# Fused causal convolution and soft mixture of experts on one core: phi's copies, the first halos, unread products, expert layers and first stores reordered

## The chip, the cores and the metric

One core of a Trainium2 chip runs the whole program. The metric is the device time in microseconds (us) of one execution, given as the median of several runs. Lower is better. The engines are PE (matrix products), DVE (vector), ACT (scalar and activation), POOL (GpSimd) and SP, which here only issues transfers; 16 DMA engines move the data. All data are fp32.

## What is computed

```python
# B, S, D = 8, 3584, 192; 8 heads of 24 channels, 7 taps; E = 8 experts, 4 slots each, F = 1024
w = softmax(weight, axis=-1)                        # one 7-tap filter per head
x_unf = x_pad[:, idx, :].reshape(B, S, K, H, group) # causal windows of 7 rows
x = einsum('hk,bskhg->bshg', w, x_unf).reshape(B * S, D)

logits = x @ phi                                    # 28672 x 32
d = softmax over the tokens (axis 0)                # dispatch weights
slot_input = (d.T @ x).reshape(E, S_per_e, D)
for e in range(E):
    slot_out[e] = maximum(slot_input[e] @ w1[e], 0.0) @ w2[e]
c = softmax over the slots (axis 1)                 # combine weights
out = c @ slot_out.reshape(n_slots, D)
```

The softmax over all 28,672 tokens stands between the convolution of every batch and the first row of the output.

## The kernel before

The eight batches of 3584 tokens lie in five buffers `rb[0..4]` of 128 partitions. A batch is 32 blocks of 112 tokens (two halves of 56, each with 8 rows of the block before it, the halo); it is loaded in four quarters of 8 blocks. `load_x` (L251) issues the transfers and then copies the halo rows of each quarter from partitions 64 on to partitions 0 on (`halo`, L272); the copy runs on ACT for two quarters of batch 0 and on POOL otherwise.

The convolution is a product with a banded matrix `toep` per head. DVE builds the bands (`bprod`, L351, a product of 392 columns, and `bsum`, L354), POOL takes the products of heads 3 and 6. A convolution group (`conv`, L408) is written to one of four PSUM pairs and evacuated over its own input (L196 on ACT, L200 on DVE). For batches 0 and 1 a group covers two heads and half of the blocks, first quarters 0 and 1, then 2 and 3; for the others one head and all blocks, which needs all four halos. DVE then transposes the result in blocks of 32 (`turn`, L452) into `xt`.

Batches are taken in units of two. The logits of a unit are six steps (`step`, L492), which need `phi4`: phi lies on 32 partitions and is copied to the other 96 by three copies (`phi_copies`, L287 to L289). The steps stand between the convolution groups of the next unit. Behind them come the evacuation with a running minimum (L517), the exponential (L532), a transpose on PE (L558) and the dispatch product (L583), whose results are merged into `acc` on DVE (L590). The combine weights are made per batch by `rows` (L601): two transposes and two reductions on DVE, two products of 1.7 us on POOL (L610), one exponential on ACT.

`filler(n)` (L432) adds n products of the identity with itself (L438, two instructions each in the order) into a PSUM pair that is about to be overwritten; nobody reads them.

When the last dispatch is done, slot sums become slot inputs `s1z`, `s2z` (L746 to L763); the first expert layer `l1` (L786) is taken in two halves h of 512 columns, each from a high part (`s1z`, L789) and a low part (`s2z`, L793); then ReLU (L802 on ACT, L804 on DVE), a transpose `ht` of each quarter q (L816) with its copy, the second layer `l2` (L827), a gather (L845) and the copy to `so` (L848). The weights are loaded into `rb[3]`, `rb[4]` (w1), `xt` and `rb[0]` (w2) once their former contents have been read (L717 to L733).

The output of a batch is made for tokens k and k + 1 of every seven at a time (L870), evacuated by ACT and DVE, one half each, and stored by four transfers per batch (`st`, L895); batch 0 is stored in two portions of four.

The order on each engine is set by `Plan` (L16 to L148): each step has a cost in us, keys that it reads and writes, and a priority; `order` places the steps at the earliest time by these costs, and among those that are ready the one of the lowest priority value first. Steps with `chain=True` keep the order in which they are added. The engines run what stands in this order, and each instruction waits for what it needs.

## Time and profile before

| | us |
|---|---|
| median of 3 runs | 212.44 (212.21 to 212.63) |
| the profiled execution | 213.65 |
| its span, first to last instruction | 211.3 |
| PE busy | 176.9 (84%) |
| DVE busy | 153.7 (73%) |
| ACT busy | 100.1 (47%) |
| POOL busy | 77.8 (37%) |

The span is what lies between the first and the last instruction on the core; 2.35 us of the profiled execution lie around it. The profile comes from one execution, so durations read from it are set against 213.65, not against the median. The views read here are the page's busy tenths (the span in 40 slices of 5.28 us), the timeline of one engine, in which equal instructions in a row are merged, and the table of stretches. A row of the timeline gives the start, the time from the first start to the last end, the engine, the line, the operation, its tiles, and in brackets how long the engine had been idle and what released it.

### The profile page before, as it was taken

How to read it: one execution, taken by the hardware profiler on the slowest of the kernel's cores; microseconds unless marked ns; L12 is line 12 of the kernel's file. 1: busy time of each engine (PE TensorE's matmuls, PEld its weight loads, DVE VectorE, ACT ScalarE, POOL GpSimd, SP SyncE). 2: the span in 40 equal slices, each digit the busy share in tenths (PEclk: the TensorE clock that was granted, in tenths of full speed). 3: DMA queues.
4: the chain of work that ended last, by engine and by line, in shares of the span. 5: the costliest groups of instructions: out<-in, count | busy, mean ns of one | idle time of the engine just before them, and what ended most of it. 6: DMA issues, size and time to landing. Idle time of an engine off the chain costs nothing. (4 is left out here: it accounts for less than half of the span.)

```text
span 211.3 us, 6138 instructions
## 1 busy us (share of the span) xinstructions
PE 176.9 (84%) x2632; PEld 109.0 (52%) x2632; DVE 153.7 (73%) x231; ACT 100.1 (47%) x156; POOL 77.8 (37%) x69
## 2 busy tenths in 40 slices
PE   7749999999999999999999989988999999680000
PEld 3235786427632375323646667333898988660000
DVE  5994797088997999978889967769789897660000
ACT  3083655075284563747882080331669779550000
POOL 7726646655345640654000602246303633300000
PEclk9978999999999999999999999999999887875555
DMA  5999999997799917999079699900199999999994
GB/s 166 326 322 326 323 330 323 325 326 238 208 330 324 310 30 218 326 380 236 21 229 304 159 352 379 356 26 0 39 337 324 399 413 401 416 412 416 415 413 193
DMA packets 46124, 60.08 MB, mean 284 GB/s; under 512 B 1682, under 2 KB 38418, under 8 KB 46098
## 3 DMA queue, kind: packets, MB, share of 16 engines
q1 hardware_dynamic: 45888, 59.68, 86.0%
q8 instruction: 20, 0.33, 0.7%
q10 hardware_dynamic: 210, 0.02, 0.1%
q14 instruction: 6, 0.05, 0.1%
HBM read 37.68 MB, written 22.02 MB: 282 GB/s over the span
## 5 line engine op out<-in xcount | busy, mean ns | idle before, releaser
L196 ACT COPY rb<-ps 128x768 f32<-128x768 f32 (+1 forms) x97 | 69.4, 783 | 50.7 <-PE ps L408 28.6
L452 DVE STREAM_TRANSPOSE xt<-rb 128x1024 f32<-128x1024 f32 (+1 forms) x60 | 57.4, 1004 | 9.4 <-ACT rb L196 6.6
L198 POOL COPY rb<-rb 8x1536 f32<-8x1536 f32 x30 | 43.7, 1457 | 40.2 <-DMA rb<-in_x_dram 39.3
L408 PE MATMUL ps<-rb,toep 64*64 64x384 f32 (+1 forms) x640 | 48.2, 432 | 5.3 <-ACT rb L196 5.3
L610 POOL TENSOR_TENSOR eb<-eb,rms 128x896 f32<-128x896 f32 x16 | 27.0, 1696 | 61.2 <-DVE rms L614 43.5
L870 PE MATMUL ps<-so,eb 32*128 32x192 f32 x448 | 38.8, 454 | 3.1 <-DVE eb L627 1.7
L870 PEld LDWEIGHTS ps<-so,eb 32*128 32x128 f32 x448 | 35.0, 318 | 7.0 <-ACT rb L196 3.3
L408 PEld LDWEIGHTS ps<-rb,toep 64*64 64x64 f32 x640 | 22.0, 134 | 30.4 <-issue 20.2
L200 DVE COPY rb<-ps 128x768 f32<-128x768 f32 (+1 forms) x31 | 25.7, 854 | 6.5 <-ACT rb L196 3.3
L492 PE MATMUL ps<-xt,phi 32*32 32x384 f32 (+1 forms) x768 | 27.4, 545 | 0.0
L583 PE MATMUL ps<-rb,xt 128*32 128x192 f32 x448 | 19.0, 327 | 0.0
L617 DVE TENSOR_REDUCE rms<-eb 128x28 f32<-128x896 f32 x16 | 16.9, 1060 | 1.9 <-ACT eb L623 1.9
L492 PEld LDWEIGHTS ps<-xt,phi 32*32 32x32 f32 x768 | 11.1, 103 | 12.6 <-issue 7.5
L583 PEld LDWEIGHTS ps<-rb,xt 128*32 128x32 f32 x448 | 14.1, 110 | 4.0 <-ACT rb L196 0.3
L438 PE MATMUL ps<-ident 128*128 128x256 f32 x48 | 14.0, 423 | 0.0
L532 ACT ACTIVATE xt<-eb,nmr 128x896 f32<-128x896 f32 x8 | 8.3, 1044 | 9.2 <-DVE eb L517 9.1
L438 PEld LDWEIGHTS ps<-ident 128*128 128x128 f32 x48 | 8.8, 200 | 4.8 <-issue 2.5
L558 PEld LDWEIGHTS ps<-ident,xt 128*128 128x128 f32 x64 | 6.9, 141 | 5.4 <-ACT xt L532 3.6
L196 ACT COPY xt<-ps 128x512 f32<-128x512 f32 (+2 forms) x12 | 6.1, 529 | 7.4 <-DVE xt L200 6.0
L558 PE MATMUL ps<-ident,xt 128*128 128x128 f32 x64 | 8.7, 280 | 1.1 <-ACT xt L532 1.1
L627 DVE STREAM_TRANSPOSE eb<-eb 128x896 f32<-128x896 f32 x8 | 8.8, 1106 | 0.1
L620 DVE STREAM_TRANSPOSE eb<-eb 128x896 f32<-128x896 f32 x8 | 8.6, 1087 | 0.0
(89 smaller groups left out, 114.7 us busy)
## 6 DMA issues: line engine op xcount, KB each, us to landing
out_dram<-rb SPq DMA_DIRECT2D x28, 672.0 KB, 9.6
rb<-in_x_dram SPq DMA_DIRECT2D x24, 768.0 KB, 9.5
rb<-in_x_dram SPq DMA_DIRECT2D x8, 672.0 KB, 7.3
rb<-in_moe_w_dram SPq DMA_DIRECT2D x4, 1024.0 KB, 10.4
xt<-in_moe_w_dram SPq DMA_DIRECT2D x4, 768.0 KB, 7.9
rb<-in_moe_w_dram SPq DMA_DIRECT2D x4, 768.0 KB, 10.7
rb<-in_moe_w_dram SPq DMA_DIRECT2D x4, 512.0 KB, 13.7
out_dram<-rb SPq DMA_DIRECT2D x4, 384.0 KB, 5.0
```

The costliest lines, as they stand in the source:

```text
L196: nc.scalar.copy(dst, src)
L198: nc.gpsimd.tensor_copy(dst, src)
L200: nc.vector.tensor_copy(dst, src)
L408: nc.tensor.matmul(dst[:, :, h * CG : (h + 1) * CG], toep[r, h0 + h, :], rb[i][r, lo + g : lo + n : 2, ch], start=True, stop=True,)
L438: lambda e: nc.tensor.matmul(prs[p][:, 0, 0 : 2 * P].rearrange("p (r n) -> p r n", n=P), ident, ident.unsqueeze(1).broadcast_to((P, 2, P)) ...
L452: nc.vector.transpose(xt[:, s, k, lo : lo + n], rb[i][:, lo : lo + n, 32 * k : 32 * k + 32])
L492: nc.tensor.matmul(q[a % 2][32 * c : 32 * c + 32, a // 2, 0 : m * U * n].rearrange("p (s u j) -> p s u j", s=m, j=n), phi4[sl, k, :], xt[s ...
L558: nc.tensor.transpose(q[:, u // 4, (u % 4) * P : (u % 4 + 1) * P], t[:, u].rearrange("p g t -> p (g t)"), ident)
L583: nc.tensor.matmul(q[32 * c : 32 * c + 32, 0, 0:D], d[:, u, 32 * c : 32 * c + 32], rb[i][:, U * c + u, :], start=(u == 0), stop=(u == U - 1),)
L610: return lambda e: veng(e).tensor_tensor(out=ev, in0=ev, in1=rb_, op=op)
L617: return lambda e: nc.vector.tensor_reduce(out=rm, in_=ev, axis=AX.X, op=op)
L870: nc.tensor.matmul(q4[c // 2][:, c % 2, (q - k) * D : (q - k + 1) * D], cb[:, :, q], so[sl, :], start=True, stop=True, tile_position=(32 * ...
```

## The change

- phi's copies to the other partitions are added behind batch 0's stage and also wait for the evacuation of batch 0's last heads; their priority goes from -2 to 12.
- Batch 0's halos of quarters 0 and 1 are on ACT (before: 1 and 2); quarters 2 and 3 on POOL.
- Fewer fillers: in the first two batches 2, 2, 2, 0 | 0, 0, 0, 2 | 0, 0, 0, 3 | 0, 0, 0, 1 (before 2, 3, 2, 1 | 0, 0, 0, 1 | 0, 0, 0, 4 | 0, 0, 0, 2), none among the first unit's logits (2), three before the last logits (4), one after the last dispatch (3).
- The expert layers are chained on PE in an order written by hand, the first layer cut into its high and low part.
- Batch 0 is stored in portions of two and five tokens (before four and three). One planned wait of two w1 loads is dropped.

```diff
--- before.py
+++ after.py
@@ -273,7 +273,7 @@
                 copy(e, rb[i][0:HR, n * q : n * (q + 1), :], rb[i][64 : 64 + HR, n * q : n * (q + 1), :])
 
             add(fn, {"DMA": n * P * D * 4 / 325e3 + (0.6 if b == q == 0 else 0)}, writes=[ldk[i][q]], after=hk[i] + [hak[i][q]], prio=pr)
-            add(halo, {"ACT": 1.5} if b == 0 and q in (1, 2) else {"POOL": 1.5}, reads=[ldk[i][q]] + ([f"z{i}"] if q == 0 else []), writes=[hak[i][q]], prio=pr)
+            add(halo, {"ACT": 1.5} if b == 0 and q < 2 else {"POOL": 1.5}, reads=[ldk[i][q]] + ([f"z{i}"] if q == 0 else []), writes=[hak[i][q]], prio=pr)
 
     def load_w(dst, src, nbytes, key, after, prio):
         add(lambda e: nc.sync.dma_start(dst, src), dma(nbytes), writes=[key], after=after, prio=prio)
@@ -332,8 +332,7 @@
     )
 
     add(w_norm, {"DVE": 0.9}, reads=["wb"], writes=["wb"], prio=-50)
-    add(phi_copies, {"ACT": 1.05}, reads=["phi0"], writes=["phi4"], prio=-2)
-
+    
     def shifts(e):
         lo, k = 2 * HR - ZS, T - HR + ZS
         nc.vector.tensor_tensor(out=shf[:, 0:k], in0=ident[:, 66 : 66 + k], in1=ident[:, lo : lo + k], op=ALU.add)
@@ -462,7 +461,7 @@
             for lo in (0, NI):
                 for h in range(0, H, 2):
                     conv(b, h, 2, lo, NI)
-                    filler(((2, 3, 2, 1), (0, 0, 0, 1), (0, 0, 0, 4), (0, 0, 0, 2))[2 * b + lo // NI][h // 2])
+                    filler(((2, 2, 2, 0), (0, 0, 0, 2), (0, 0, 0, 3), (0, 0, 0, 1))[2 * b + lo // NI][h // 2])
                 for k in range(NB):
                     turn(b, s, k, lo, NI)
         else:
@@ -641,19 +640,19 @@
                     for h, n in enumerate(ld):
                         between[h] = [lambda z=z: step(z) for z in range(k, k + n)]
                         k += n
-                    if j == 1:
-                        between[0].append(lambda: filler(2))
                     between[len(ld) - 1].append(done)
                     between[len(ld) + 1] = [lambda: state.update(held=())]
                 between[H - 1] = [lambda: turn_d(prev[0])]
             stage(b, s, between)
+            if b == 0:
+                add(phi_copies, {"ACT": 1.05}, reads=["phi0", hk[0][6] + ".1"], writes=["phi4"], prio=12)
             if s == 0 and prev:
                 turn_d(prev[1])
                 dispatch(prev[0])
                 if j < len(units) - 1:
                     dispatch(prev[1])
     unit = units[-1]
-    filler(4)
+    filler(3)
     step, done = logits(unit)
     for k in range(NB):
         step(k)
@@ -701,7 +700,7 @@
 
     for v in unit:
         dispatch(v)
-    filler(3)
+    filler(1)
 
     FQ = F // 4
     FH = F // 2
@@ -721,7 +720,7 @@
         for a in range(2):
             load_w(
                 w1h[h][64 * a : 64 * a + 64, E:], w1[a::2, P:D, fs].rearrange("q p f -> p q f"), P * FH * 8,
-                w1k[h][2 + a], allk(3 + h) + (xk0 if h else []), 1003 + 4 * h + a,
+                w1k[h][2 + a], allk(3 + h), 1003 + 4 * h + a,
             )
     for q in range(4):
         for z in range(2):
@@ -781,22 +780,27 @@
     add(mt4, {"DVE": 0.5}, reads=["ri", "mask", "gsel"], writes=["sel"], after=["dn1.0", "dn1.1"], prio=pr + 5)
 
     hp = [prs[(pd, pa)[h]][:, 0, :] for h in range(2)]
-    for h in range(2):
-
-        def l1(e, h=h):
-            for a in range(2):
+    op = prs[pc][:, 1, 0 : 2 * D].rearrange("p (a d) -> p a d", d=D)
+
+    def l1(h, low):
+        def fn(e):
+            for a in range(0 if low else 2):
                 for g in range(G):
                     nc.tensor.matmul(
                         hp[h][g * NS : (g + 1) * NS], s1z[a], w1h[h][:, 2 * g + a], start=(a == 0), stop=False
                     )
-            for g in range(G):
+            for g in range(G if low else 0):
                 nc.tensor.matmul(hp[h][g * NS : (g + 1) * NS], s2z, w1h[h][:, E + g], start=False, stop=True)
 
-        add(l1, {"PE": 2.6}, reads=["s1z", "s2z"] + w1k[h], writes=[f"p{(pd, pa)[h]}"], prio=pr + 1)
-
+        add(
+            fn, {"PE": 0.9 if low else 1.75}, reads=["s2z" if low else "s1z"] + (w1k[h][2:] if low else w1k[h][:2]),
+            writes=[f"p{(pd, pa)[h]}"], prio=pr + 1, chain=True,
+        )
+
+    def relu(h):
         for z in range(2):
 
-            def relu(e, h=h, z=z):
+            def fn(e, z=z):
                 o, i_ = hs[:, 2 * h + z], hp[h][:, z * FQ : (z + 1) * FQ]
                 if e == "ACT":
                     nc.scalar.activation(o, i_, AF.Relu)
@@ -804,24 +808,28 @@
                     nc.vector.tensor_scalar(out=o, in0=i_, scalar1=0.0, scalar2=None, op0=ALU.max)
 
             add(
-                relu, {"ACT": 0.41} if z else {"DVE": 0.4}, reads=[f"p{(pd, pa)[h]}"], writes=[f"hs{2 * h + z}"],
+                fn, {"ACT": 0.45} if z else {"DVE": 0.42}, reads=[f"p{(pd, pa)[h]}"], writes=[f"hs{2 * h + z}"],
                 after=["xt3.1"], prio=pr + 2,
             )
-    op = prs[pc][:, 1, 0 : 2 * D].rearrange("p (a d) -> p a d", d=D)
-    for q in range(4):
+
+    def turn_h(q):
         tv = prs[pb][:, q % 2, 0 : 2 * P].rearrange("p (j n) -> p j n", n=P)
 
-        def ht(e, q=q, tv=tv):
+        def ht(e):
             for j in range(2):
                 nc.tensor.transpose(tv[:, j, :], hs[:, q, j::2], ident)
 
-        add(ht, {"PE": 0.25}, reads=[f"hs{q}"], writes=[f"ht{q % 2}"] + ([f"p{pb}", "mtb"] if q == 0 else []), prio=pr + 0.5 + (1 if q > 1 else 0))
         add(
-            lambda e, q=q, tv=tv: copy(e, hT[:, q], tv), {"ACT": 0.41} if q % 2 else {"DVE": 0.4},
+            ht, {"PE": 0.33}, reads=[f"hs{q}"], writes=[f"ht{q % 2}"] + ([f"p{pb}", "mtb"] if q == 0 else []),
+            prio=pr + 1, chain=True,
+        )
+        add(
+            lambda e: copy(e, hT[:, q], tv), {"ACT": 0.45} if q % 2 else {"DVE": 0.42},
             reads=[f"ht{q % 2}"], writes=[f"hT{q}"], after=["xt2.1"], prio=pr + 3,
         )
 
-        def l2(e, q=q):
+    def l2(q):
+        def fn(e):
             for j in range(2):
                 for g in range(G):
                     nc.tensor.matmul(
@@ -831,9 +839,23 @@
                     )
 
         add(
-            l2, {"PE": 1.4}, reads=[f"hT{q}"] + [f"w2.{q}.{z}" for z in range(2)],
-            writes=["op"], after=[f"p{pc}"] if q == 0 else [], prio=pr + 1.6,
-        )
+            fn, {"PE": 1.33}, reads=[f"hT{q}"] + [f"w2.{q}.{z}" for z in range(2)],
+            writes=["op"], after=[f"p{pc}"] if q == 0 else [], prio=pr + 1, chain=True,
+        )
+
+    l1(0, False)
+    l1(0, True)
+    relu(0)
+    l1(1, False)
+    turn_h(0)
+    turn_h(1)
+    l1(1, True)
+    relu(1)
+    l2(0)
+    turn_h(2)
+    turn_h(3)
+    for q in range(1, 4):
+        l2(q)
     for a in range(2):
         add(
             lambda e, a=a: copy(e, oc[a], op[:, a]), {"ACT": 0.36} if a else {"DVE": 0.33},
@@ -888,8 +910,8 @@
                     oev, {"ACT": act(2 * nq * D), "DVE": dve(2 * nq * D)}, reads=[pk[j]], writes=[f"ob{b % 4}.{j}.{k}"],
                     after=obk[b] if b < 4 else [], prio=pr + k,
                 )
-            if (b == 0 and k == 2) or k == 6:
-                k0 = 4 if b == 0 and k == 6 else 0
+            if (b == 0 and k == 0) or k == 6:
+                k0 = 2 if b == 0 and k == 6 else 0
                 for c in range(4):
 
                     def st(e, c=c, b=b, ob=ob, k0=k0, k1=k + nq):
```

On ACT, at the start of the program (`rb_67` is batch 0, `rb_68` batch 1; 8x1536 is a halo copy):

```order
 L328 ACTIVATE wb<-wb 128x56
 L330 DMA phi_85<-in_moe_phi_dram 32x6x32
-L289 COPY phi_85<-phi_85 32x192 x3
 L196 COPY rb_67<-rb_67 8x1536 x2
 L196 COPY rb_67<-ps_63 128x16x48
```

Phi's copies stood ahead of the two halos; now nothing stands between phi's transfer and the halos.

On ACT again, among the evacuations of batch 1:

```order
 L196 COPY rb_68<-ps_65 128x16x48
 L196 COPY rb_68<-ps_66 128x16x48
+L289 COPY phi_85<-phi_85 32x192 x3
 L196 COPY rb_68<-ps_63 128x16x48
 L196 COPY rb_68<-ps_64 128x16x48
```

Here they stand now, between the last evacuation of the first half and the first of the second.

On PE, from the last dispatch to the second expert layer, before (`ps_66` and `ps_63` hold the first layer's halves, `ps_64` the transposes, `ps_65` the second layer):

```order
L583 MATMUL ps_66<-rb_69,xt 32x192 x32
L438 MATMUL ps_63<-ident 128x256 x3
L746 MATMUL ps_64<-gself,acc 128x32
L750 MATMUL ps_64<-gself,acc 64x32 x2
L754 MATMUL ps_65<-dtot,gself 32x1 x4
L789 MATMUL ps_66<-rb_70,s1z_90 32x512 x4
L789 MATMUL ps_66<-rb_70,s1z_91 32x512 x4
L793 MATMUL ps_66<-rb_70,s2z 32x512 x4
L789 MATMUL ps_63<-rb_71,s1z_90 32x512 x4
L789 MATMUL ps_63<-rb_71,s1z_91 32x512 x4
L793 MATMUL ps_63<-rb_71,s2z 32x512 x4
L816 MATMUL ps_64<-ident,xt 128x128 x8
```

and now, from the fillers on:

```order
L437 MATMUL ps_63<-ident 128x256
L753 MATMUL ps_65<-dtot,gself 32x1 x4
L745 MATMUL ps_64<-gself,acc 128x32
L749 MATMUL ps_64<-gself,acc 64x32 x2
L793 MATMUL ps_66<-rb_70,s2z 32x512 x4
L789 MATMUL ps_63<-rb_71,s1z_90 32x512 x4
L789 MATMUL ps_63<-rb_71,s1z_91 32x512 x4
L820 MATMUL ps_64<-ident,xt 128x128 x4
L793 MATMUL ps_63<-rb_71,s2z 32x512 x4
L835 MATMUL ps_65<-xt 32x384 x2
```

The transposes of the first half moved ahead of the second half's low part; the other four stand behind the first group of the second layer. The divisor's product (L754, now L753) moved ahead of the slot products.

## Rows read from the trace of the kernel before

**Rows 1.** The page's busy tenths: PE, granted clock, GB/s in 40 slices.

```profile
PE   7749999999999999999999989988999999680000
...
PEclk9978999999999999999999999999999887875555
...
GB/s 166 326 322 326 323 330 323 325 326 238 208 330 324 310 30 218 326 380 236 21 229 304 159 352 379 356 26 0 39 337 324 399 413 401 416 412 416 415 413 193
```

**Rows 2.** Timelines of ACT and of the DMA queue where the stores begin.

```profile
149.15 1.67 ACT L196 COPY rb<-ps 128x768 f32<-128x768 f32 x2 [0.64 <-PE ps L870]
...
150.88 49.44 SPq L899 DMA_DIRECT2D out_dram<-rb  x36
```

**Rows 3.** Timeline of PE from the first convolution to batch 2.

```profile
13.53 1.51 PE L408 MATMUL ps<-rb,toep 64*64 64x192 f32 x16 [4.46 <-ACT rb L196]
...
34.49 5.50 PE L492 MATMUL ps<-xt,phi 32*32 32x512 f32 x160
39.93 1.13 PE L438 MATMUL ps<-ident 128*128 128x256 f32 x4
40.99 0.88 PE L408 MATMUL ps<-rb,toep 64*64 64x384 f32 x8
```

**Rows 4.** Timeline of PE: batch 4, last logits, last fillers, expert layers.

```profile
63.30 0.88 PE L408 MATMUL ps<-rb,toep 64*64 64x384 f32 x8
...
111.06 1.99 PE L438 MATMUL ps<-ident 128*128 128x256 f32 x8
112.98 6.56 PE L492 MATMUL ps<-xt,phi 32*32 32x512 f32 x192
...
130.64 1.56 PE L438 MATMUL ps<-ident 128*128 128x256 f32 x6
...
132.04 0.30 PE L746 MATMUL ps<-gself,acc 128*128 128x32 f32 x2
...
134.60 1.04 PE L793 MATMUL ps<-rb,s2z 128*32 128x512 f32 x8
...
139.81 0.74 PE L816 MATMUL ps<-ident,xt 128*128 128x128 f32 x4 [0.92 <-ACT xt L196]
```

**Rows 5.** Timeline of ACT before the first evacuation.

```profile
10.86 1.07 ACT L289 COPY phi<-phi 32x192 f32<-32x192 f32 x3 [6.03 <-DMA phi<-in_moe_phi_dram]
11.96 2.84 ACT L196 COPY rb<-rb 8x1536 f32<-8x1536 f32 x2
```

**Rows 6.** Load of quarter 1 of batch 0: issue (start us) and landing.

```profile
L270 SPq DMA_DIRECT2D rb<-in_x_dram x1: 563/563/563, 1.7 to 1.7; - x1
...
DMA to landing us min/median/max: 6.5/6.5/6.5
```

**Rows 7.** Timeline of DVE while it builds the bands.

```profile
6.01 1.80 DVE L351 TENSOR_TENSOR xt<-shf,wb 128x392 f32<-128x392 f32 x1
...
12.47 0.56 DVE L351 TENSOR_TENSOR xt<-shf,wb 128x392 f32<-128x392 f32 x1
...
14.01 1.29 DVE L351 TENSOR_TENSOR xt<-shf,wb 128x392 f32<-128x392 f32 x1
```

**Rows 8.** Timeline of POOL: last halos of batches 2 and 4.

```profile
33.81 1.46 POOL L198 COPY rb<-rb 8x1536 f32<-8x1536 f32 x1 [0.94 <-DMA rb<-in_x_dram]
...
53.80 1.46 POOL L198 COPY rb<-rb 8x1536 f32<-8x1536 f32 x1
```

**Rows 9.** Timeline of DVE: last logits, last dispatch, first ReLU.

```profile
118.84 1.05 DVE L620 STREAM_TRANSPOSE eb<-eb 128x896 f32<-128x896 f32 x1
...
130.78 0.41 DVE L590 SCALAR_TENSOR_TENSOR acc<-acc,alt,ps 128x192 f32<-128x192 f32 x1 [0.20 <-PE ps L583]
...
135.90 0.36 DVE L804 TENSOR_SCALAR xt<-ps 128x256 f32<-128x256 f32 x1
```

**Rows 10.** Two stretches: length, busy per engine, clock, DMA share, GB/s.

```profile
13.70:17.10 3.40, 3.40 (x24) 2.03 (x23) 2.87 (x4) 1.90 (x2) 2.55 (x2) 0.51 1.10 326
...
152.00:154.00 2.00, 1.76 (x27) 1.79 (x30) 1.12 (x3) 0.90 (x3) 0.00 (x0) 1.00 0.93 255
```

## The prediction

> **What bounds the kernel now.** Read the busy tenths first [rows 1]: PE is at 8 or 9 in nearly every slice from the 4th to the 34th, and from the 30th on the DMA engines move 324 to 417 GB/s until the last slice. So there are two stages, a PE stage and a store stage that begins before PE is done. Then the store stage: the DMA queue issues its first store at 150.88, right behind two evacuations on ACT that began at 149.15 [rows 2]; it is one of 36, and the trace ends at 211.3 with nothing but stores. The span is therefore the time of the first store plus about 60.4 us (211.3 - 150.88), and what counts is how much earlier the first store is issued. Before it, `so` needs everything: all logits, the eight dispatches, the expert layers. In that stage PE waits for nobody for long except in two places, at 13.53 (4.46 us behind ACT) and at 139.81 (0.92 us) [rows 3, 4]. The third view to read is therefore what PE did between those two waits that nobody reads, and what would be late next if PE were not.
>
> **The front: phi's copies, first halos, fillers.** The first convolution starts at 13.53 and was released by ACT [rows 3]. ACT stood before phi's copies for 6.03 us, copied phi for 1.07, and only then copied the two halos, 2.84 for both [rows 5]. The second of them (quarter 1) could have started when its load landed: issued at 1.7, landed 6.5 later, at 8.2 [rows 6]. In the changed order ACT copies quarter 0 (landed earlier) and quarter 1 at once, POOL does not touch either, so the second halo ends at 8.2 + 1.42 = 9.6 and PE starts near 9.8, with the lag of 0.15 seen before (13.53 after 11.96 + 1.42 = 13.38). That is 3.7 us earlier.
> The bands must keep up. DVE's first product took 1.80 instead of 0.56, and the last one 1.29, both beside a halo copy on POOL [rows 7]. Now POOL's own two products start at once, and its halos of quarters 2 and 3 fall into DVE's middle. The first two bands take two products and two sums: four operations of about 0.5 from 6.01 and at most 0.8 of blocking each, 9.6 at the latest, so in time. The last band cannot be expected earlier than before (1.29 at 14.01, then its sum: 15.9), because the same halo of quarter 3 stands beside it; PE reaches that band near 16, so this costs nothing, and up to 1.3 in the rival below.
> Then the length of PE's front. Before, the 16 convolution groups and 15 fillers from 13.53 to the logits at 34.49 took 20.96 [rows 3]. The change drops three fillers; a filler is two products of 1.99 / 8 = 0.25 [rows 4], so 3 x 0.5 = 1.5, and 19.5 remain at most (before, the first group ran at half clock, 1.51 against 0.88 for as many columns at 40.99; if it runs at full clock now, still less). Logits then start by 9.8 + 19.5 = 29.3, their five steps take 5.5 (34.8), the filler of 1.13 behind them at 39.93 is gone, and PE stands before batch 2 at 34.8 instead of 40.99. What is late next: batch 2's last halo, a copy on POOL of 1.46 that started at 33.81 behind its load [rows 8], 35.27. The loads of batches 0 to 4 run back to back at 320 to 330 GB/s from the start [rows 1], nothing in the change moves them, so this is a floor: PE starts batch 2 near 35.4 and the gain is 40.99 - 35.4 = **5.6**, with 0.5 to 2 us of slack in front of it. This is the largest term, and it is set by a load, not by how many fillers went.
> Does the shift survive to the first store? Batch 4 is the next fixed date: its last halo ends at 53.80 + 1.46 = 55.26 [rows 8], and PE would reach batch 4 at 63.30 - 5.6 = 57.7 [rows 4]: 2.4 to spare. Later batches load into buffers that PE itself frees, so their dates move with it, and so do the weights', whose transfers are over in the 27th slice while the stores begin in the 29th [rows 1].
> Phi's copies now sit on ACT between the evacuations of batch 1's halves, 1.07 us. Queued behind them is the second half's first evacuation. Three fillers (1.5) stand there on PE and four PSUM pairs rotate, which hides them; without that cover it would be 1.07, inside the same slack.
>
> **The middle: filler and transpose before the last logits' evacuation.** The fillers ahead of the last logits go from four to three: 0.5 (1.99 for eight) [rows 4]. The logits end at 112.98 + 6.56 = 119.54; DVE was in a transpose of 1.05 that began at 118.84 [rows 9] and took the evacuation only after it, 0.35 late. In the new order that transpose stands behind the expert layer's inputs. Sum **0.8**; bounds 0.3 and 0.9.
>
> **The fillers after the last dispatch**, three to one: PE is in them from 130.64 for 1.56, while DVE finishes `acc` at 130.78 + 0.41 = 131.19 [rows 4, 9]. One filler (0.52) ends about there, so the slot products can start near 131.3 instead of 132.04. DVE gets its two small steps on the divisor ahead of the copies of `s1z`, some 0.3. I take **0.55** between 0 (DVE late by these steps and a POOL product beside them) and 0.7.
>
> **The expert layers.** The same products in another order. Before, four transposes of both halves stood together and PE waited 0.92 for ACT's copy between them [rows 4]. Now the second half's low part lies over the first copies, and the first second-layer group over the second ReLU. A ReLU takes 0.36 on DVE, a copy about the same, the low part that covers the first copies 1.04 [rows 4, 9]; that is enough if DVE is not in one of its row operations of 1.05. I take **0.9**, between 0 (a row operation stands ahead of a copy on DVE) and 0.95.
>
> **First stores of two tokens.** The first store waits for one evacuation per engine instead of two: half of 1.67 [rows 2], 0.84 earlier. But the four short stores carry half the bytes, and the five-token stores behind them wait for the same last evacuations as before. The first 2 us of stores moved only 255 GB/s [rows 10]; part of the lead will be lost to that slow start. **0.6**, between 0 and 0.84. Bytes and the number of stores stay, so the rest of the 60.4 stays.
>
> **Sum.** 5.6 + 0.8 + 0.55 + 0.9 + 0.6 = 8.45. The profiled execution took 213.65 (span 211.3), so it would take 205.2. The median of the runs is 1.21 lower, 212.44; from it 204.0. By their bounds the terms after the front add from 0.3 to 3.4 instead of 2.85, so 203.5 to 206.5 with the front as it stands; a load that lands half a microsecond off moves that by as much.
>
> **Rivals.**
> *A stretch at half clock.* PE has fewer products that nobody reads and a new wait of 0.5 to 2 us before batch 2. [...] Against it: idle stretches of under 1 us later left the clock alone [rows 1, 4]. [...] 15%.
> *The ends do not arrive.* DVE's row operations stand before copies, and short stores bring nothing: the last three terms, 2.05, vanish, 206.1. For it: DVE has such operations of 1.05 between its small steps [rows 9]. 10%.
> *The bands come late.* If POOL's halos block two more of DVE's products, 0.7 to 1.2 each, the front is late by 2, its slack of 0.5 is spent: 1.5 less, 205.5. 8%.
> *Slower than before: the front stays at half clock.* [...] At 1.51 / 0.88 = 1.7 the 19.5 become 33 and five steps 9.4: batch 2 at 52.2, 11.2 later than now, less the 2.85 of the rest: 220.8. It is slower than before from about 22 us at half clock ((40.99 + 2.85 - 34.8) / (1 - 1/1.7)). Against it: the fall at slice 3 healed within one stretch at the present density, and the convolution groups stay back to back. 3%.
> *It does not do what it says*: ACT's second halo still waits for something else and PE starts at 13.5. Then 19.5 + 5.5 lead to 38.5, a front gain of 2.5: 207.1. 3%.
>
> **How the numbers follow.** Forecast 204.0, 59%. The rivals at 205.4, 206.1 and 205.5 (33%) lie within the range; 203.5 is the lower bound of the terms, and 0.7 for loads and store rate goes below it: 202.8 to 206.7. Outside are 207.1, 220.8 and what I have not seen, 8% and more. A measurement of this kernel can tell about 0.2% (0.4 us) from no change; all cases but the slower one and a sum of several are beyond that: faster 94%, same 2%, slower 4%.
>
> **What would show it.** First convolution near 9.8, not 13.5; a PE wait of 0.5 to 2 us that ends at a POOL halo near 35.3; no granted clock below full between 10 and 40; last logits ending near 113; no PE wait over 0.4 within the expert layers; first store near 142.6 and the end some 60 us behind it. It is wrong if batch 2 starts after 37, or if the stretch from first store to end grows by over 1 us.

## The result

| | before | changed |
|---|---|---|
| median of four runs, us | 212.53 | 206.59 |
| lowest to highest run | 212.21 to 214.89 | 206.39 to 208.12 |
| the profiled execution | 213.65 | 206.39 |
| its span | 211.3 | 204.6 |

The ratio is 0.9713, with a 95% interval of 0.963 to 0.9796. The forecast was 204.0 in a range from 202.8 to 206.7: the sign and the range hold, the size is 2.6 us off. The median lies 0.1 inside the upper end of the range, and that end had been set so high for causes that did not come, so that the range holds is in part luck. The page of the changed kernel (engines, then busy tenths in 40 slices, then the queue of instructions) answers to [rows 1]:

```profile
PE 173.8 (85%) x2616; PEld 104.8 (51%) x2616; DVE 152.7 (75%) x230; ACT 100.7 (49%) x157; POOL 78.0 (38%) x69
...
PE   7999899799999999998999999998999977972000
...
PEclk9999999999999999999999999999999998555555
...
GB/s 155 326 321 330 321 329 324 325 323 326 321 320 332 269 22 261 338 382 186 52 252 297 189 382 374 352 17 0 153 325 358 405 411 410 408 414 415 413 416 187
...
q8 instruction: 20, 0.33, 0.7%
```

The dip of the granted clock in slices 3 and 4 is gone, and the loads of batches 0 to 4 run as before. The front of PE, which answers to [rows 3] (timeline: start, length, engine, line, operation, tiles, count, idle time before it and what ended it):

```profile
9.85 0.88 PE L407 MATMUL ps<-rb,toep 64*64 64x192 f32 x16
...
25.83 2.83 PE L407 MATMUL ps<-rb,toep 64*64 64x192 f32 x64 [0.95 <-POOL rb L198]
...
29.22 5.99 PE L491 MATMUL ps<-xt,phi 32*32 32x512 f32 x160
35.36 0.88 PE L407 MATMUL ps<-rb,toep 64*64 64x384 f32 x8 [0.15 <-POOL rb L198]
36.17 1.07 PE L491 MATMUL ps<-xt,phi 32*32 32x512 f32 x13
38.17 1.09 PE L491 MATMUL ps<-xt,phi 32*32 32x512 f32 x19 [0.94 <-issue]
39.20 1.52 PE L407 MATMUL ps<-rb,toep 64*64 64x384 f32 x16
```

The first convolution comes at 9.85 instead of 13.53, and batch 2's first group at 35.36 instead of 40.99, released by the POOL halo. That is 5.63 earlier, as forecast. The same place in the kernel before:

```profile
41.79 1.14 PE L492 MATMUL ps<-xt,phi 32*32 32x512 f32 x32
42.86 1.54 PE L408 MATMUL ps<-rb,toep 64*64 64x384 f32 x16
```

The sixth logits step, 1.07 us from its start to batch 2's second group in the kernel before, takes from 36.17 to 39.20 in the changed one. Behind its 13th pass PE stands still, and the releaser is "issue": PE waits for nothing that the profile shows. The weight loads of PE in the same stretch:

```profile
31.36 0.42 PEld L491 LDWEIGHTS ps<-xt,phi 32*32 32x32 f32 x32 [0.78 <-issue]
32.00 0.93 PEld L491 LDWEIGHTS ps<-xt,phi 32*32 32x32 f32 x34 [0.22 <-issue]
33.10 1.41 PEld L491 LDWEIGHTS ps<-xt,phi 32*32 32x32 f32 x39 [0.17 <-issue]
35.36 0.21 PEld L407 LDWEIGHTS ps<-rb,toep 64*64 64x64 f32 x8 [0.85 <-POOL rb L198]
36.17 0.17 PEld L491 LDWEIGHTS ps<-xt,phi 32*32 32x32 f32 x13 [0.60 <-issue]
38.17 0.20 PEld L491 LDWEIGHTS ps<-xt,phi 32*32 32x32 f32 x19 [1.84 <-issue]
```

Between the idle time that ends at 31.36 and the one that ends at 38.17 lie 32 + 34 + 39 + 8 + 13 = 126 loads; the trace has 127 product passes and three waits for a semaphore beside them, 256 records of PE. The second group of batch 2 is 3.66 earlier than before, not 5.6. From there the lead is kept: the last logits, the expert layers and the first output product in the changed kernel, against [rows 4]:

```profile
108.82 6.56 PE L491 MATMUL ps<-xt,phi 32*32 32x512 f32 x192
...
126.27 0.70 PE L437 MATMUL ps<-ident 128*128 128x256 f32 x2
...
127.99 1.92 PE L789 MATMUL ps<-rb,s1z 128*32 128x512 f32 x16 [0.28 <-DVE s1z L757]
...
132.42 0.74 PE L820 MATMUL ps<-ident,xt 128*128 128x128 f32 x4
133.10 1.07 PE L793 MATMUL ps<-rb,s2z 128*32 128x512 f32 x8
...
142.10 2.18 PE L892 MATMUL ps<-so,eb 32*128 32x192 f32 x32 [0.54 <-DVE so L870]
```

The lead is 4.16 at the last logits (112.98 to 108.82), and 0.5 of that is the filler. The two rows of L820 and L793 stand without any idle time where the kernel before had 0.92. On the queue of the transfers the first store comes at 144.29 instead of 150.88 [rows 2] (forecast near 142.6), a lead of 6.59, and the end lies 60.3 behind it (60.43 before):

```profile
144.29 49.97 SPq L921 DMA_DIRECT2D out_dram<-rb  x36
```

So every term arrived near its size but the first, which gave 2.0 us back within one step. The experiments ask what PE waited for there.

### The profile page after: what moved, and what is told of

It reads as the page before. It is cut to its first block, busy times and chain, and to the rows that moved or that the text cites. A ratio compares the mean times of both kernels' runs of the same rounds, so it can differ in the third digit from the quotient of the medians.

```text
span 204.6 us, 6095 instructions
## 1 busy us (share of the span) xinstructions
PE 173.8 (85%) x2616; PEld 104.8 (51%) x2616; DVE 152.7 (75%) x230; ACT 100.7 (49%) x157; POOL 78.0 (38%) x69
## 3 DMA queue, kind: packets, MB, share of 16 engines
q1 hardware_dynamic: 45888, 59.68, 88.6%
## 4 chain that ended last, share of the span: by engine, by line
PE 47%; DMA 12%; SPq 11%; DVE 9%; ACT 5%; POOL 5%; issue 3%; DVEq 0%; ACTq 0%; POOLq 0%
DMA rb<-in_x_dram 12%; PE ps L407 10%; PE ps L892 10%; SPq L270 9%; PE ps L582 8%; PE ps L491 7%; PE ps L557 4%; POOL eb L609 3%; PE ps L835 3%; SPq L266 2%; ACT rb L196 2%; DVE rms L616 2%; DVE rb L200 2%; PE ps L789 2%; POOL rb L198 1%
## 5 line engine op out<-in xcount | busy, mean ns | idle before, releaser
L451 DVE STREAM_TRANSPOSE xt<-rb 128x1024 f32<-128x1024 f32 (+1 forms) x60 | 56.8, 1000 | 5.1 <-ACT rb L196 2.4
L407 PE MATMUL ps<-rb,toep 64*64 64x384 f32 (+1 forms) x640 | 47.6, 427 | 2.4 <-POOL rb L198 1.1
L892 PEld LDWEIGHTS ps<-so,eb 32*128 32x128 f32 x448 | 34.2, 318 | 9.5 <-DVE eb L626 3.6
L200 DVE COPY rb<-ps 128x768 f32<-128x768 f32 (+1 forms) x30 | 25.0, 856 | 8.7 <-PE ps L892 8.4
L491 PE MATMUL ps<-xt,phi 32*32 32x512 f32 (+1 forms) x768 | 28.7, 545 | 0.9 <-issue 0.9
L622 ACT ACTIVATE eb<-eb 128x896 f32<-128x896 f32 x8 | 7.6, 954 | 3.4 <-POOL eb L609 3.3
L309 PE MATMUL ps<-ident 128*128 128x512 f32 x10 | 8.0, 959 | 1.4 <-POOL ident masks.py:199 1.4
L437 PE MATMUL ps<-ident 128*128 128x256 f32 x32 | 9.0, 405 | 0.0
L626 DVE STREAM_TRANSPOSE eb<-eb 128x896 f32<-128x896 f32 x8 | 8.8, 1104 | 0.1
## 6 DMA issues: line engine op xcount, KB each, us to landing
rb<-in_moe_w_dram SPq DMA_DIRECT2D x4, 512.0 KB, 14.5
```

Source lines behind the costliest of these rows:

```text
L200: nc.vector.tensor_copy(dst, src)
L407: nc.tensor.matmul(dst[:, :, h * CG : (h + 1) * CG], toep[r, h0 + h, :], rb[i][r, lo + g : lo + n : 2, ch], start=True, stop=True,)
L451: nc.vector.transpose(xt[:, s, k, lo : lo + n], rb[i][:, lo : lo + n, 32 * k : 32 * k + 32])
L491: nc.tensor.matmul(q[a % 2][32 * c : 32 * c + 32, a // 2, 0 : m * U * n].rearrange("p (s u j) -> p s u j", s=m, j=n), phi4[sl, k, :], xt[s ...
L892: nc.tensor.matmul(q4[c // 2][:, c % 2, (q - k) * D : (q - k + 1) * D], cb[:, :, q], so[sl, :], start=True, stop=True, tile_position=(32 * ...
```

## Experiments

Theory F: PE ran out of instructions. The page counts 2616 products and 2616 weight loads, and 20 packets of instructions with 0.33 MB, so 262 instructions for each packet of 16 KB. Counting all of the trace's records of PE (loads, products and waits for a semaphore) from the first on, PE of the changed kernel stands still behind the 449th, the 705th and the 961st, 256 apart each. Such a wait is given below from the start of the last instruction ahead of it to the next start (0.5, 0.5 and 1.5 here); the idle time in a row begins only when the last product has ended, and is some 0.6 shorter. Theory R: the sixth step waits for something of its own. Each group of runs has its own runs of the kernel before; medians of the kernel before differ by up to 0.8 us between groups, so the position of a wait says more than a total.

**Old fillers in the changed kernel.**

```diff
-((2, 2, 2, 0), (0, 0, 0, 2), (0, 0, 0, 3), (0, 0, 0, 1))
+((2, 3, 2, 1), (0, 0, 0, 1), (0, 0, 0, 4), (0, 0, 0, 2))
...
+                    if j == 1:
+                        between[0].append(lambda: filler(2))
```

> The changed kernel with the unread products of the front put back as before (2, 3, 2, 1 | 0, 0, 0, 1 | 0, 0, 0, 4 | 0, 0, 0, 2 and two behind the first logits): five fillers, 2.5 us of PE work, more than in the changed kernel. Theory F: in the changed kernel PE ran out of instructions in the sixth logits step (36.17 to 39.20 for 1.07 us of work), because its instructions come in blocks of 256 and the next block takes 6 to 7 us from the moment PE enters the last one it has. Then the fillers mostly take the place of waiting: batch 2's first group moves from 35.36 to about 37.5, the sixth step no longer waits more than 0.5, batch 2's second group starts at 39.4 to 40.0 (changed kernel 39.20), time 0.2 to 0.8 over the changed kernel's 206.6. Theory R: the sixth step waits for something of its own, whatever stands before it; then the 1.9 us of waiting stay and the second group starts near 41.5, time near 208.9.

PE's timeline in this kernel:

```profile
36.31 0.88 PE L407 MATMUL ps<-rb,toep 64*64 64x384 f32 x8
37.11 1.27 PE L491 MATMUL ps<-xt,phi 32*32 32x512 f32 x32
38.32 1.52 PE L407 MATMUL ps<-rb,toep 64*64 64x384 f32 x16
```

The wait is gone and the second group comes at 38.32, which is 0.88 earlier than in the changed kernel, with 2.5 us more of work in front of it. Theory R expected 41.5. The gain is even larger than F expected (39.4 to 40.0). The time was 206.90 (before 213.07; ratio 0.973, 0.9686 to 0.9774), within the spread of the changed kernel's own: in this profiled run the store stage was 0.9 longer. By these totals, taking fillers out of the front brought nothing by itself.

**No fillers in the front.**

```diff
-((2, 2, 2, 0), (0, 0, 0, 2), (0, 0, 0, 3), (0, 0, 0, 1))
+((0, 0, 0, 0), (0, 0, 0, 0), (0, 0, 0, 0), (0, 0, 0, 0))
```

> The changed kernel without any unread product among the first 16 convolution groups (12 fillers fewer, 48 PE instructions fewer; the lead-in products stay). Theory F: batch 2's first group stays at 35.4, set by its load; the block that was missing begins 48 instructions later in the program, about at the end of the sixth step, so PE meets it at 37.1 or later instead of 36.65 and the block itself is asked for earlier; the second group starts at 37.3 to 38.2 instead of 39.20, time 204.7 to 205.7. Theory R (the sixth step waits for something of its own): nothing changes after 35.4, 206.6. [...]

Neither F nor R alone: 210.52 (before 213.07; 0.9882, 0.9843 to 0.992), slower than the changed kernel. The granted clock in 40 slices of 5.22 us and a stretch (length, busy per engine with counts, clock, DMA share, GB/s), then PE's timeline in the front and in the last logits:

```profile
PEclk9985999999999999999999799999999997678555
...
116.06:119.20 3.14, 3.14 (x58) 1.02 (x60) 0.00 (x0) 0.00 (x0) 0.45 (x1) 0.64 0.25 22
```

```profile
13.44 1.02 PE L407 MATMUL ps<-rb,toep 64*64 64x192 f32 x16 [1.50 <-DVE toep L353]
15.93 8.39 PE L407 MATMUL ps<-rb,toep 64*64 64x192 f32 x136 [1.46 <-DVE toep L353]
```

```profile
108.29 4.94 PE L491 MATMUL ps<-xt,phi 32*32 32x512 f32 x138
116.06 3.17 PE L491 MATMUL ps<-xt,phi 32*32 32x384 f32 x54 [2.83 <-issue]
```

Without fillers PE stands idle for two bands, 1.50 and 1.46, and the granted clock falls behind the first of these waits: it is at half from 14.5 to 21.3 us (the dip in slices 3 and 4). The front has room for that: batch 2 still starts at 35.32, and its second group at 37.20, close to what F expected (37.3 to 38.2), though PE then waits 1.0 within it, at the 961st instruction. The 4 us are lost elsewhere, in the last logits: PE waits 3.4 in the middle of them (2.83 of it idle), again at "issue" and again at such an instruction, 449 + 12 x 256 = 3521, and runs on at a lower clock (0.64 over the next 3.1 us). So the granted clock did fall in the front, but that is not where the time went. The same wait thus opened here at a second stage, in which PE used up 138 passes in 4.94 us.

**Sixty instructions more in the lead-in,** where PE waits anyway; all engines keep their order.

```diff
+        def lead_in(e, i=i):
+            if i < 4:
...
+                return
+            for c in range(4):
+                for a in range(4):
+                    sl, sc = slice(32 * a, 32 * a + 32), slice(32 * c, 32 * c + 32)
+                    nc.tensor.matmul(
+                        prs[2 * (a % 2)][sc, a // 2, 0:32], ident[sl, sc], ident[sl, 0:32], start=True, stop=True,
+                        tile_position=(32 * a, 32 * c),
+                    )
```

> The changed kernel with the last lead-in product (4 PE instructions, before the first convolution, where PE waits anyway) replaced by 16 tiny ones (64 instructions). All else stands in the same order on each engine. Theory F: whatever PE waits for at a block's end comes 60 instructions earlier in the program: the wait of 1.5 us that stands behind the 13th pass of the sixth step (45 of 64 instructions are behind it) moves ahead into the end of the fifth step or just before it, ahead of batch 2's first group, which then starts near 37; the sixth step takes under 1.6 instead of 3.03; the second group starts within 0.6 of 39.2 and the time is within 0.6 of 206.6. Theory R: the wait stays in the sixth step behind the same pass, batch 2's first group stays at 35.4.

```profile
29.30 5.90 PE L501 MATMUL ps<-xt,phi 32*32 32x512 f32 x160
35.34 0.88 PE L417 MATMUL ps<-rb,toep 64*64 64x384 f32 x8
36.14 1.14 PE L501 MATMUL ps<-xt,phi 32*32 32x512 f32 x32
37.22 1.54 PE L417 MATMUL ps<-rb,toep 64*64 64x384 f32 x16
```

The sixth step takes 1.14, against R. But the wait did not move into the fifth step as F expected, it went: the second group is at 37.22, 1.98 earlier, and the time 205.87 (before 213.07; 0.9658, 0.9613 to 0.9703). The packet with the missing block started 2.0 us after PE had entered the block before it, where the changed kernel's took 4.3 (table below). Why it came earlier is not known.

**Loads of batches 3 and 4 held back.**

```diff
+            if b == 3 and q == 0:
+                add(
+                    lambda e: copy(e, rb[3][32:40, 0, 0:8], rb[2][32:40, 16, 0:8]), {"POOL": 0.1},
+                    reads=[ldk[2][2], hak[2][2]], writes=["hold"], prio=-9,
+                )
-            add(fn, {"DMA": n * P * D * 4 / 325e3 + (0.6 if b == q == 0 else 0)}, writes=[ldk[i][q]], after=hk[i] + [hak[i][q]], prio=pr)
+            add(fn, {"DMA": n * P * D * 4 / 325e3 + (0.6 if b == q == 0 else 0)}, reads=["hold"] if 2 < b < NR else [], writes=[ldk[i][q]], after=hk[i] + [hak[i][q]], prio=pr)
```

> The changed kernel with the loads of batches 3 and 4 held back until POOL has copied the third halo of batch 2 (a copy of 8 by 8 elements into batch 3's buffer that the loads then wait for), so that the DMA engines run dry for one or two us near 34. Theory F with the loads as the reason why the instruction block comes late: the 16 KB packet of instructions that started at 35.68 starts by 34.2, PE finds its instructions, the sixth step takes 1.1 to 1.4 instead of 3.03 and batch 2's second group starts at 37.2 to 37.8 instead of 39.20. Batch 3 has some 7 us to spare; batch 4's last halo comes 1 to 2.5 later than 57.1, against a need near 57.6, so PE waits there and the time gains 0 to 1 only. Theory R, or blocks that come late for another reason than the loads: the sixth step still takes about 3, and the time is 206.6 or more.

Stretches of the changed kernel first (from the entry into the last block at hand, through the packet, to PE's restart), then the first stretch of this kernel, then its PE:

```profile
31.35:35.68 4.33, 4.18 (x114) 2.29 (x113) 0.09 (x1) 0.00 (x0) 2.92 (x2) 1.00 1.10 320
35.68:36.83 1.15, 1.15 (x21) 0.17 (x13) 0.00 (x0) 0.48 (x1) 0.53 (x1) 1.00 1.09 329
36.83:38.17 1.34, 0.41 (x6) 0.00 (x0) 0.00 (x0) 0.32 (x1) 0.93 (x1) 1.00 1.09 329
```

```profile
31.34:32.42 1.08, 1.08 (x40) 0.65 (x36) 0.08 (x1) 0.00 (x0) 0.78 (x1) 1.00 0.33 100
```

```profile
35.25 0.88 PE L412 MATMUL ps<-rb,toep 64*64 64x384 f32 x8
36.06 1.14 PE L496 MATMUL ps<-xt,phi 32*32 32x512 f32 x32
37.13 1.54 PE L412 MATMUL ps<-rb,toep 64*64 64x384 f32 x16
...
58.50 0.88 PE L412 MATMUL ps<-rb,toep 64*64 64x384 f32 x8 [0.87 <-POOL rb L198]
```

With the DMA engines at 100 GB/s instead of 320 the packet starts 1.08 after the entry instead of 4.33, the wait is gone, and the second group comes at 37.13, as expected under F. PE's instructions and their order are those of the changed kernel, so it was the loads that delayed the block here. The other packets bear this out: in all 14 traces together, 40 packets started while the engines moved under 100 GB/s of data (from the entry to the packet's start, 1 us at least), at most 1.6 after the entry; 196 started at 300 GB/s or more, up to 5.8 after it, the median at 3.2. The gain of 2.07 did not last: batch 4 then comes late (the wait of 0.87 at 58.50), and two later waits for instructions, at the 2753rd and the 3521st, cost 1.15 and 0.8. The time is 206.36 (before 213.07; 0.97, 0.9656 to 0.9745).

The block that begins behind the 961st record in each of these traces, in us (entry and "is through" are the starts of the first and the last instruction of the block before it):

| kernel | PE enters the block before it | packet starts | packet ends | PE is through the block before | PE waits |
|---|---|---|---|---|---|
| before | 35.74 | 38.55 | 39.69 | 41.81 | 0 |
| changed | 31.35 | 35.68 | 36.83 | 36.65 | 1.5 |
| old fillers | 31.07 | 34.79 | 35.94 | 37.25 | 0 |
| 60 more | 29.66 | 31.67 | 32.84 | 34.15 | 0 |
| loads held | 31.34 | 32.42 | 33.47 | 36.12 | 0 |

Wherever PE waited at this block, it went on 1.3 to 1.6 after the packet's end. So in the changed kernel a block needed 4.33 + 1.15 + 1.34 = 6.8 us from the entry into the one before it, and a step of logits uses up 64 instructions in 1.07 us, a block in 4.3.

**The front as before,** all else changed: phi's copies, halos and fillers back (the first three points of the change undone, the tail's fillers not).

```diff
-{"ACT": 1.5} if b == 0 and q < 2 else {"POOL": 1.5}
+{"ACT": 1.5} if b == 0 and q in (1, 2) else {"POOL": 1.5}
...
+    add(phi_copies, {"ACT": 1.05}, reads=["phi0"], writes=["phi4"], prio=-2)
...
-((2, 2, 2, 0), (0, 0, 0, 2), (0, 0, 0, 3), (0, 0, 0, 1))
+((2, 3, 2, 1), (0, 0, 0, 1), (0, 0, 0, 4), (0, 0, 0, 2))
```

> The changed kernel with its whole front as before: phi's copies ahead of the halos, halos of quarters 1 and 2 on ACT, five fillers more. The rest stays changed. By the traces of both kernels the front is worth 3.7 (batch 2's second group at 42.86 before, 39.20 after), not the 5.6 predicted: expected 210.0 to 210.7, batch 2's second group within 0.2 of 42.9, and no wait for instructions over 0.3 up to there. If the three other parts are worth less than the 3.0 that the traces show, the time is over 211.

210.10 (before 212.79; 0.9894, 0.986 to 0.9928), the second group at 42.52, 0.4 earlier than expected. So the three other parts are worth 2.7 by the medians (2.9 by the two first traces), and the front brought what the second group's place says, 3.3 to 3.7, and not 5.6.

**The tail's fillers as before.**

```diff
-    filler(3)
+    filler(4)
...
-    filler(1)
+    filler(3)
```

> The changed kernel with four fillers ahead of the last logits and three behind the last dispatch, as before. The prediction gives these two edits 0.5 (plus 0.35 by a transpose on DVE) and 0.55: the first expert product comes 0.9 to 1.4 later than its 127.99, time 0.9 to 1.4 over the changed kernel's 206.6. Rival: DVE, not PE, sets both places (the divisor's steps and the last merge), then the fillers are covered and the time rises by 0.3 at most. These 12 instructions more also move the ends of the 256-instruction blocks behind them, which may cost or spare up to 1 us of waiting in the last logits or dispatches.

209.68 (before 212.79; 0.9861, 0.9829 to 0.9892). The first expert product is 2.40 later than in the changed kernel. Of that, 1.27 stood there already at batch 7's first group, from a wait for instructions at the 2753rd (449 + 9 x 256) that the changed kernel's first trace lacks; the rest, 1.13, is the fillers: 0.43 at the last logits, 0.20 up to the dispatch, 0.50 behind the last one. By the trace the fillers' part is within what was expected, against the rival's 0.3. The time rose by more than the expected 0.9 to 1.4: 209.68 against medians of 206.59 and 207.97 for the changed kernel in other groups.

**The expert layers in the old order** (one uncut `l1` for each half, its four transposes together behind both).

```diff
-    l1(0, False)
-    l1(0, True)
-    relu(0)
-    l1(1, False)
-    turn_h(0)
-    turn_h(1)
-    l1(1, True)
...
+        add(l1, {"PE": 2.6}, reads=["s1z", "s2z"] + w1k[h], writes=[f"p{(pd, pa)[h]}"], prio=pr + 1)
```

> The changed kernel with the expert layers in the old order (first layer uncut, four transposes together). The prediction gives the new order 0.9, the trace 0.85: PE waits near 0.9 for ACT's copy between the transposes, the first output product comes 0.7 to 1.0 later counted from the first expert product (14.96 before, 14.11 after), the time rises by 0.7 to 1.0. Rival: the gain stood in DVE's row operations that the new order moves behind the small steps, and they only come later elsewhere: then the first output product is late but the end is not, within 0.2.

```profile
133.65 0.74 PE L815 MATMUL ps<-ident,xt 128*128 128x128 f32 x4
135.31 0.75 PE L815 MATMUL ps<-ident,xt 128*128 128x128 f32 x4 [0.92 <-ACT xt L196]
```

The wait of 0.92 is back [rows 4], and the first output product comes 15.08 behind the first expert product instead of 14.11: 0.97. The time is 208.95 (before 212.79; 0.9794, 0.9739 to 0.9848; this interval overlaps the changed kernel's). The end is later too, against the rival: from the first expert product it is 78.4 away, in the changed kernel's two traces 76.6 and 76.3.

**The first stores as before,** and a second group with the changed kernel beside it, on both bases.

```diff
-            if (b == 0 and k == 0) or k == 6:
-                k0 = 2 if b == 0 and k == 6 else 0
+            if (b == 0 and k == 2) or k == 6:
+                k0 = 4 if b == 0 and k == 6 else 0
```

> The changed kernel with batch 0 stored in portions of four and three tokens as before. PE, DVE, ACT and POOL run the same order. The prediction gives the short stores 0.6 between 0 and 0.84; by the traces the first store was issued 0.87 earlier and the stretch from there to the end stayed (60.43 before, 60.3 after): first store near 145.1 instead of 144.29, time 0.6 to 0.9 higher. Rival: what bounds the end is the rate of all stores behind the sixth or so, the early ones only fill a slow start: the first store comes later, the end within 0.3.

> The changed kernel itself once more, beside the three others of this group, since times of different groups differ by up to 1 us. Expected 206.4 to 207.6; the wait in the sixth logits step again between 1.3 and 1.8 behind the same 13th pass, whatever the total.

> The changed kernel with batch 0 stored in portions of four and three tokens, once more. In the first look the first store came 1.22 later, 0.34 of it from before the output stage, and the last byte only 0.28 later. Theory E (the end is set by the last output groups and the rate of the later stores, the early lead only fills a slow start): time within 0.3 of the changed kernel in this group. Theory P (the prediction): 0.6 to 0.9 slower.

> The changed kernel with the 16 tiny products in the lead-in, once more. Its trace had batch 2's second group at 37.22 (changed kernel 39.20), and PE waited for instructions later at three places, 0.3 to 0.5 each. Expected 0.8 to 2.0 below the changed kernel in this group, batch 2's second group at 37.1 to 37.6. If the block comes as late as in the changed kernel (4.3 behind the point where it can be asked for, instead of 2.0), the wait of 1.5 to 2.5 stands at the end of the fifth step and the gain is gone.

> The kernel with the 16 tiny products and batch 0 stored in portions of four and three tokens: the second pair for the stores. Theory E: within 0.3 of the kernel with the 16 tiny products. Theory P: 0.6 to 0.9 slower than it.

| kernel | median, us | ratio to before, 95% interval | first output product to end, profiled run |
|---|---|---|---|
| changed | 207.97 | 0.9704 (0.964 to 0.9767) | 62.20 |
| changed, stores of 4 and 3 | 208.64 | 0.976 (0.971 to 0.981) | 63.15 |
| 60 more | 205.08 | 0.9616 (0.9563 to 0.967) | 62.35 |
| 60 more, stores of 4 and 3 | 206.42 | 0.9662 (0.9608 to 0.9717) | 63.80 |

The kernel before had 213.31 in this group. The stores of two tokens are worth 0.67 and 1.34 by the medians, 0.95 and 1.45 by the profiled runs; but the first run with the old stores (208.15; before 212.79; 0.9801, 0.9772 to 0.9831) gave 62.47 in its trace, the same as the changed kernel's first trace (62.51). Two pairs of three thus speak for theory P, with intervals that overlap: the term is likely above zero, and its size is not settled. The changed kernel's own median here, 207.97, lies above the 206.4 to 207.6 that was expected of it. The kernel with 60 instructions more is the fastest of all in both of its groups, here by 2.9, more than the 0.8 to 2.0 that was expected; its interval overlaps that of the changed kernel, its traces were 2.0 and 3.6 shorter than the changed kernel's two.

The two "60 more" traces and the changed kernel's second one also show where the wait goes. First the kernel with 60 more and the old stores, then the changed kernel again, in the sixth step and in a later one:

```profile
29.27 5.43 PE L501 MATMUL ps<-xt,phi 32*32 32x512 f32 x152
35.42 1.05 PE L501 MATMUL ps<-xt,phi 32*32 32x512 f32 x8 [0.71 <-issue]
36.40 0.88 PE L417 MATMUL ps<-rb,toep 64*64 64x384 f32 x8
37.21 1.14 PE L501 MATMUL ps<-xt,phi 32*32 32x512 f32 x32
```

```profile
36.19 1.07 PE L491 MATMUL ps<-xt,phi 32*32 32x512 f32 x13
38.40 1.09 PE L491 MATMUL ps<-xt,phi 32*32 32x512 f32 x19 [1.15 <-issue]
```

```profile
88.74 1.12 PE L491 MATMUL ps<-xt,phi 32*32 32x512 f32 x28
90.61 1.04 PE L491 MATMUL ps<-xt,phi 32*32 32x512 f32 x4 [0.75 <-issue]
```

In the first, the packet started 3.1 after the entry, and the wait of 1.3 stands behind 152 passes of the logits: that is the place that F had named, 160 + 8 + 13 - 152 = 29 passes, so 58 instructions, ahead of the changed kernel's. With the second run of the same front (packet 2.0 after the entry, wait of 0.2, second group at 37.67) this shows that the place follows the count of instructions, and the length of the wait the moment at which the packet gets through. The changed kernel's front met the wait at the 961st in all six traces that have it with its loads (1.4 to 1.7), and here another of 1.3 at the 2753rd, which its first trace did not have. Runs of this kernel from 205.71 to 208.38 in one group are thus no surprise; that these waits make all of that spread was not shown.

## Why the prediction was right, and where it was not

*Front: right up to batch 2, then wrong.* ACT copied the halos at once, and the first convolution came at 9.85 for a forecast of 9.8:

```profile
5.85 1.47 ACT L196 COPY rb<-rb 8x1536 f32<-8x1536 f32 x1 [1.01 <-DMA rb<-in_x_dram]
8.18 1.47 ACT L196 COPY rb<-rb 8x1536 f32<-8x1536 f32 x1 [0.86 <-DMA rb<-in_x_dram]
```

The logits began at 29.22 (at most 29.3), batch 2's first group at 35.36 (35.4), set by the halo. The slack of 0.5 before it was only 0.15, since the five steps took 5.99 instead of 5.5; the smaller waits at the 449th and the 705th instruction lie in that front, and so does a wait of 0.95 for a halo on POOL (25.83), which the prediction does not have. The step that failed is the sentence that the gain, once there, lasts unless batch 4 comes late: the sum took PE's time as its work and its waits for data, and left out that its instructions have to arrive too (1.5 us of waiting behind the 961st). The term was 5.6 and measured 3.7. The sign that it named, batch 2 after 37, looks at the first group and could not show this; the end of the last logits could, 115.4 for a forecast near 113. With the loads held back, or with the blocks' ends moved, the second group came at 37.1 and 37.2, 5.6 to 5.7 earlier than before: the term was right for a PE that has its instructions.

*Fillers.* "Set by a load, not by how many fillers went" was right as far as the halo: without any filler batch 2's first group came at 35.32, no earlier than with those that were left. With all of the old ones back it came at 36.31, 0.95 later, and the second group still 0.88 earlier. What they do besides was not seen: each spends 0.5 us on four instructions, and so gives the next block time (no wait at the 961st with all of the old ones, 1.5 with those that were left), and they cover the wait for the bands (1.50 and 1.46 without them).

*Middle, last fillers, expert layers, stores.* Forecast 0.8, 0.55, 0.9 and 0.6; in the first trace 0.63, 0.50, 0.85 and 0.87. Three were undone, the first two in one run, and came back at 0.63 (0.43 and 0.20), 0.50 and 0.97; the stores gave 0.7 to 1.3 by medians, with one trace that shows nothing.

*The sum against the median.* By the profiled runs the gain is 7.26 for 8.45: the front's 1.9 is missing, 0.5 came from what lies around the span (2.35 to 1.8). By the medians it is 5.94. The prediction took 1.21 off because the kernel before's profiled run lay that far above its median; the changed kernel's lay 0.2 below its own. That subtraction was worth as much as a term and rested on one run.

*Rivals.* The granted clock was 1.00 up to the first store (0 to 144.2 us), so there was no half-clock stretch in that part of the changed kernel. The 205.4 in the forecast's list counts a loss of 1.4 us for one such stretch, the author's estimate from the 3.40 us at a clock of 0.51 in the kernel before [rows 10], where a group took 1.51 for 0.88 [rows 3]; no run shows that term. What the runs showed in its place is the kernel without any fillers: its granted clock was at half from 14.5 to 21.3 us, from behind a wait of 1.50 on, and batch 2's first group still came at 35.32. The bands came at 15.8, and PE did not wait for them. The ends arrived.

## What to carry to other kernels

Where an engine runs many short instructions while the DMA engines are full, count its instructions as well as its time. Here the logits used up a block of 256 in 4.3 us, the next one needed 6.8 with the engines at 320 to 329 GB/s, and 2.0 of a gain of 5.6 us went back at the 961st instruction, with no releaser in the profile but "issue". Before work is made denser, look at where these ends fall; moving them by 60 instructions in a place where the engine waits anyway was worth 2.0 and 3.6 us here by the traces, and 1.2 and 1.9 us by the ratios to the kernel before, whose intervals overlap; in a third trace with the same front the wait came back at another place. Work that nobody needs may be what pays for that wait (with the old fillers back, batch 2's second group came 0.88 earlier), so take it out piece by piece and look at later stages too.

## What the runs showed of the hardware

Instructions of PE travel on the same DMA engines as the data, by the page's list of queues (q8 instruction: 20 packets, 0.33 MB, 0.7% of the 16 engines, beside 88.6% for the data on q1), in packets of 16 KB that take 0.9 to 1.9 us. Packets of the first 45 us, with loads at 314 to 338 GB/s, started 1.8 to 5.8 us behind PE's entry into the block before; with the engines at 100 GB/s it was 1.08. Three packets near 46 us came only 0.8 to 1.1 behind it at 325 to 330 GB/s. So full engines can delay a packet and do not always do so; what sets the delay under the same load stays open. The block of 256 is what these traces give: 262 instructions for each packet, and waits behind the 449th, the 705th and the 961st record. The waits cost 1.5 us at the 961st instruction and 3.4 in the last logits of the kernel without fillers. In these traces no packet started more than 1.0 us before PE entered the block ahead of the one that it brought.
